# Reordering the opening of an attention-plus-MLP kernel: dummy matmuls, contiguous rows, other load order, alternating heads

## The chip, the cores and the metric

The kernel runs on one NeuronCore of a Trainium2 chip. The metric is device time in microseconds (us), median of repeated runs; every timed run here is on one core. Runs whose time lay within 1.5% of the fastest of their kernel count as fast. A single look: one run, no repeats. A difference counts as faster or slower here only beyond 2%.

The measured time of a run is some 1.8 us longer than the span that its profile draws (1246.06 against 1244.3).

## The reference

```
mod = silu(c) @ w_mod                      # c: 1x448, w_mod: 448x2688, cut in six: sa, ca, ga, sb, cb, gb
h = layernorm(x) * (1 + ca) + sa           # x: 2048x448
q = h @ wq                                 # 16 heads of 256
p = softmax(q @ k_cache^T / 16)            # per head: 2048 x 2048
x = x + ga * ((p @ v_cache) @ wo)
h = layernorm(x) * (1 + cb) + sb
x = x + gb * ((gelu(h @ w_gate) * (h @ w_up)) @ w_down)    # inner width 1792
```

Everything is bf16 in memory. K and V are inputs (a cache); only q is projected.

## The kernel before

The kernel cuts attention into 64 **units**, one for each head `h` and each row block `r` of 512 rows. A unit has 16 steps `j`, one for each 128 rows of K: two matmuls for the scores `st`, the exponential `E` on ScalarE (ACT), two matmuls for the output `oT`, and a running sum `esum` on VectorE (DVE). Scores run two steps ahead of outputs. All other work (layer norm of later row blocks, Q projections, loads, the output projection `wo`) is put into the step stream as **fills**, which are attached to a pair (u, j) of unit and step.

```
# start: loads in order. SP's queue first, then (after exp(-c)) ACT's queue
load_x(nc.sync, 0); load_wm(0, WA)              # x rows 0..511; first 960 columns of w_mod
wq[0] = load_wq(0); kTs[0] = load_k(0, parts=2) # K transposed by the DMA, in two halves
load_x(nc.sync, 2); load_wm(WA, 3 * D); wos[0] = load_wo(0)
load_x(nc.sync, 3); wq[1] = load_wq(1)
... # cps: c turned into a column by four tiny matmuls; sg = exp(-c)
load_x(nc.scalar, 1); vs[0] = load_v(0, nc.scalar)   # 1 MB of V, all at once
...
def q_proj(h, r):            # one head, one row block: 8 full matmuls
    for dc in range(2):
        qps = mi_tile([P, 512], F32, "qps")
        for ch in range(DCH):    # the fourth 128-row slice holds only 64 rows of weights
            nc.tensor.matmul(qps[:], lhsT=wq[h][:, ch, ...], rhs=hr[:, ch, :], ...)
        # half 0 copied out by DVE, half 1 by ACT
...
for t in range(4):           # row block 0
    if t == 1:
        silu_c(); modc = mod_cols(0)   # 32 tiny matmuls give sa and ca as columns
    ln.stats(t)
    if t % 2 == 1: ln.rstd(t - 1, 2)   # 1/sqrt on GpSimd (POOL)
mod_cols_out(modc, sa_c, ca1p_c)
for t in range(4): ln.norm(t)
ln.twin(nc.vector)
for pr in range(2): ln.transpose(pr)   # 16 transposes on TensorE, then modulation
q_proj(0, 0)

units = [(h, r) for h in range(H) for r in range(NC)]   # head by head
...   # row block r of head 0 needs hT of block r, so blocks 1, 2, 3 are normalised,
...   # turned (2 and 3 through DRAM) and projected inside units 0, 1 and 2
for u, (h, r) in enumerate(units):
    for j in range(NKS):
        g = u * NKS + j
        emit_st(g + 2); emit_exp(g + 1)
        ... # esum, then the two oT matmuls of step g
        for f in fills.pop((u, j), ()): f()
        if j == 7: pinv = psums()                    # 1/sum of the unit before
        if j in (9, 11, 13, 15): wo_tile(...)        # output projection of the unit before
```

The sums of a unit take a trip: `esum` goes to DRAM (`scr`), comes back transposed (`esT`), and DVE reduces it to `inv` at step 7 of the next unit.

The softmax here doesn't subtract the row's maximum and nothing guards it: scores larger than these inputs give would overflow.

## Time and profile before

| reading, kernel before | value | view |
|---|---|---|
| time, median | 1246.06 us (13 runs, 1244.86 to 1247.25) | runs |
| span of the profile | 1244.3 us | page |
| TensorE busy | 98% of the span | page |
| first score matmul starts | 14.43 us | TensorE timeline |
| last group of Q projections of heads 0 to 2 starts | 159.97 us | TensorE timeline |
| the stretch between them | 145.54 us | difference |
| from there to the end of the span | 1084.3 us | difference |

The kernel can only be faster where TensorE (PE in the profile) is idle or does work that can be dropped. The page of the kernel before, cut to the lines that say so; "9" in the clock row means 90% or more of full clock granted in that fortieth of the span:

```profile
span 1244.3 us, 17140 instructions
...
PE 1221.8 (98%) x5786; PEld 550.5 (44%) x5900; DVE 796.7 (64%) x1682; ACT 715.2 (57%) x1217; POOL 77.7 (6%) x93
...
PEclk9999999999999999999999999999999999999999
...
PE 93%; DVE 3%; issue 1%; DMA 1%; POOL 1%; ACT 0%; DVEq 0%; ACTq 0%; POOLq 0%
```

The second line is busy time by engine; the last one divides the chain of waits that ended last among the engines. PE has 93% of it. PE is idle for 22.5 us of the span (1244.3 less 1221.8); the 7% of the chain that lie elsewhere are more than that, because the chain may pass through another engine while PE is busy with something else. An upper limit for what filling holes can give is the 22.5 us, and the true one is lower: this profile lacks 114 of PE's records (5786 matmuls for 5900 weight loads), and time without a record counts as idle. The timeline of PE in the kernel before shows that start (columns: start, length, engine, source line, operation, output<-inputs, shapes, count, and in brackets the idle time before it with what ended it):

```profile
2.10 0.26 PE L167 MATMUL cps<-ones_col,c_row 1*128 1x1 bf16 x4 [2.10 <-DMA c_row<-in_c_dram]
6.70 0.24 PE L190 MATMUL modc<-scT,wm 128*128 128x1 bf16 x3 [4.33 <-DMA wm<-in_w_mod_dram]
7.19 0.93 PE L190 MATMUL modc<-scT,wm 128*128 128x1 bf16 x29 [0.25 <-DMA wm<-in_w_mod_dram]
9.13 2.49 PE L278 MATMUL tp<-id_bf,xn 128*128 128x128 bf16 x16 [1.00 <-POOL rs L232]
11.41 0.63 PE L304 MATMUL qps<-hT,wq_t 128*128 128x512 bf16 x1
12.21 2.30 PE L304 MATMUL qps<-hT,wq_t 128*128 128x512 bf16 x6 [0.17 <-ACT hT L291]
14.43 0.38 PE L345 MATMUL st<-qT,kT 128*128 128x512 bf16 x1
15.19 0.59 PE L345 MATMUL st<-qT,kT 128*128 128x512 bf16 x2 [0.38 <-ACT qT L311]
```

A lone 512-column matmul shows 0.38 us in this view, but matmuls overlap, so two take 0.59 us and follow each other every 0.216 us when the array runs at full speed (in the whole timeline twelve start one after the other from 17.13 to 19.72 us). Four of the six matmuls of the projection at 12.21 us take 1.65 us in the chain of waits, 0.41 us each: half speed, called cold below, as full speed is called warm. The clock row does not show it: it reads full from the first slice on, because it counts the time before the first clock record as full. The packed trace itself (the array `0/clock` of trace.npz) has its first record, a rise to full clock, at 13.52 us, and the last two of the six, from 13.92 us in the chain, take 0.61 us together, as two at full speed do.

After the start come holes. The waits of PE in the kernel before, from its first score matmul to 91 us (engine, line, what it waited for: sum in us, times, longest):

```profile
PE oT L538 <- DVE oTn L501: 1.0, 1, 1.0
PE st L345 <- ACT qT L311: 0.8, 2, 0.4
PE qps L304 <- DVE hT L266: 0.7, 2, 0.4
PE oT L538 <- ACT E L495: 0.5, 2, 0.3
PE st L345 <- DVE qT L309: 0.4, 1, 0.4
PE tp L278 <- POOL xn L242: 0.3, 1, 0.3
```

These are 3.7 us with a named cause. Counting the matmuls of this stretch at their full-speed spacing gave 6.0 us of holes in all (the prediction shows the count); the rest is spread in pieces for which the profile names no releaser. All of the named waits but one (0.38 us for the second half of q at 15.19) come while row blocks 1 to 3 are brought into play and head 0 is already running.

One more line of the kernel before, from the timeline of the weight loads (PEld), which are the first readers of K:

```profile
14.72 0.10 PEld L345 LDWEIGHTS <-kT 128*128 128x128 bf16 x1 [0.48 <-DMA kT<-in_A_k_cache_dram]
```

The second half-depth of K's first tile arrives at 14.7 us, just before it is wanted at 15.19. If only q were ready earlier, the scores would still wait for K (as they do for 1.49 us in before with dummies, below).

### The profile page before, as it was taken

The numbers are of one execution on the slowest core, as the hardware profiler recorded it, in microseconds if no ns is written. First come the engines' busy times: TensorE is split into PE (matmuls) and PEld (weight loads), VectorE is DVE, ScalarE is ACT, GpSimd is POOL, SyncE is SP. The second block draws the span as 40 slices with busy tenths as digits, with TensorE's granted clock in tenths as the row PEclk, the third lists the DMA queues.
The fourth block names the chain that finished last, engine by engine and source line by source line (L and its number), as shares of the span: only waits on it lengthen the run. The fifth ranks groups of instructions, "written<-read, shape, count | busy, mean of one in ns | idle before, by whom it ended". The sixth has DMA issues, their size and how long they took to land.

```text
span 1244.3 us, 17140 instructions
## 1 busy us (share of the span) xinstructions
PE 1221.8 (98%) x5786; PEld 550.5 (44%) x5900; DVE 796.7 (64%) x1682; ACT 715.2 (57%) x1217; POOL 77.7 (6%) x93
## 2 busy tenths in 40 slices
PE   7999999999999999999999999999999999999998
PEld 3444444444444444444444444444444444444443
DVE  6766666666666666676666666666666666776543
ACT  4556666666666666666666666666666666652222
POOL 4200000000000010020202010000000000000000
PEclk9999999999999999999999999999999999999999
DMA  7354031332423031402222221304041220030110
GB/s 189 87 133 97 18 67 52 47 115 51 119 43 98 22 93 43 101 18 52 63 47 67 51 67 38 81 13 97 18 86 32 49 53 18 18 85 16 50 49 16
DMA packets 181866, 76.48 MB, mean 61 GB/s; under 512 B 150161, under 2 KB 172242, under 8 KB 181778
## 3 DMA queue, kind: packets, MB, share of 16 engines
q1 hardware_dynamic: 180720, 73.87, 25.1%
q10 hardware_dynamic: 1058, 1.51, 0.4%
q8 instruction: 46, 0.75, 0.3%
q14 instruction: 42, 0.34, 0.1%
HBM read 33.67 MB, written 13.37 MB: 38 GB/s over the span
## 4 chain that ended last, share of the span: by engine, by line
PE 93%; DVE 3%; issue 1%; DMA 1%; POOL 1%; ACT 0%; DVEq 0%; ACTq 0%; POOLq 0%
PE oT L538 34%; PE st L345 34%; PE wps L354 7%; PE qps L332 6%; PE dps L592 3%; PE g_ps L579 3%; PE u_ps L579 3%; PE qps L326 1%; PE g_ps L572 1%; DVE esum L535 1%; DVE bst L224 1%; PE qps L304 0%; DMA esT<-scr 0%; DMA scr<-esum 0%; DMA x_all<-in_A_x_dram 0%
## 5 line engine op out<-in xcount | busy, mean ns | idle before, releaser
L495 ACT ACTIVATE E<-st 128x512 bf16<-128x512 f32 x1024 | 607.8, 598 | 312.3 <-PE st L345 307.0
L538 PE MATMUL oT<-E,v_h 128*128 128x512 bf16 x2005 | 599.7, 379 | 4.0 <-DVE oTn L501 1.0
L345 PE MATMUL st<-qT,kT 128*128 128x512 bf16 x2001 | 599.1, 379 | 3.9 <-ACT qT L311 0.8
L535 DVE TENSOR_TENSOR esum<-esum,E 128x512 bf16<-128x512 bf16 x896 | 396.4, 442 | 163.4 <-ACT E L495 136.4
L538 PEld LDWEIGHTS <-v_h 128*128 128x128 bf16 x2048 | 199.6, 98 | 246.2 <-DVE oTn L501 10.8
L345 PEld LDWEIGHTS <-kT 128*128 128x128 bf16 x2048 | 200.2, 98 | 228.8 <-issue 1.3
L359 DVE SCALAR_TENSOR_TENSOR x_acc<-wps,inv,x_acc 128x448 f32<-128x448 f32 x240 | 163.7, 682 | 145.3 <-PE wps L354 145.3
L354 PE MATMUL wps<-wo_t,oTn 128*128 128x448 bf16 x512 | 138.6, 352 | 0.5 <-DVE x_acc L359 0.3
L140 POOL TENSOR_TENSOR wo_t<-wo_t,ga_bf 128x448 bf16<-128x448 bf16 x32 | 34.9, 1112 | 913.1 <-DMA wo_t<-in_A_wo_dram 452.4
L584 ACT ACTIVATE gl<-g_ps 128x512 bf16<-128x512 f32 x56 | 33.4, 597 | 89.6 <-PE g_ps L579 85.5
L332 PE MATMUL qps<-hT,wq_t 128*128 128x512 bf16 x348 | 81.3, 380 | 0.6 <-issue 0.3
L354 PEld LDWEIGHTS <-oTn 128*128 128x128 bf16 x512 | 50.1, 98 | 60.9 <-issue 0.6
L337 DVE CAST qT<-qps 128x512 bf16<-128x512 f32 x60 | 41.4, 691 | 36.3 <-PE qps L332 36.1
L502 ACT CAST oTn<-oT 128x512 bf16<-128x512 f32 x64 | 37.4, 585 | 45.0 <-PE oT L538 45.0
L339 ACT CAST qT<-qps 128x512 bf16<-128x512 f32 x60 | 35.1, 585 | 46.9 <-PE qps L332 46.9
L585 DVE TENSOR_TENSOR hhT<-gl,u_ps 128x512 bf16<-128x512 bf16 x56 | 38.4, 687 | 36.1 <-PE u_ps L579 36.1
L332 PEld LDWEIGHTS <-wq_t 128*128 128x128 bf16 x360 | 32.7, 98 | 48.1 <-issue 12.7
L579 PEld LDWEIGHTS <-wgu 128*128 128x128 bf16 x336 | 30.6, 98 | 44.8 <-issue 11.9
L514 DVE TENSOR_REDUCE inv<-esT 128x4 f32<-128x512 bf16 x64 | 43.4, 679 | 4.5 <-DMA esT<-scr 4.5
L579 PE MATMUL u_ps<-hT,wgu 128*128 128x512 bf16 x165 | 45.2, 379 | 0.3
L501 DVE CAST oTn<-oT 128x512 bf16<-128x512 f32 x64 | 44.1, 689 | 0.9 <-PE oT L538 0.9
L579 PE MATMUL g_ps<-hT,wgu 128*128 128x512 bf16 x160 | 43.9, 380 | 0.8 <-issue 0.8
(71 smaller groups left out, 316.1 us busy)
## 6 DMA issues: line engine op xcount, KB each, us to landing
scr<-esum SPq DMA_DIRECT2D x64, 128.0 KB, 2.0
wo_t<-in_A_wo_dram SPq DMA_DIRECT2D x16, 224.0 KB, 6.3
wq_t<-in_A_wq_dram SPq DMA_DIRECT2D x16, 192.0 KB, 5.1
xscr<-xn SPq DMA_DIRECT2D x6, 512.0 KB, 2.9
out_dram<-ob SPq DMA_DIRECT2D x16, 112.0 KB, 1.7
wd<-in_B_w_down_dram SPq DMA_DIRECT2D x2, 784.0 KB, 4.8
x_all<-in_A_x_dram SPq DMA_DIRECT2D x3, 448.0 KB, 4.4
wgu<-in_B_w_gate_dram SPq DMA_DIRECT2D x1, 1344.0 KB
```

Source lines behind the costliest of these rows:

```text
L332: nc.tensor.matmul(qps[:], lhsT=wq[h][:, ch, dc * P:(dc + 1) * P], rhs=hT[("a", r)][:, ch, :], start=False, stop=(ch == 2),)
L337: nc.vector.tensor_copy(out=qTs[(h, r)][:, dc, :], in_=qps[:])
L345: nc.tensor.matmul(st[:], lhsT=kTs[h][:, dc, j * P:(j + 1) * P], rhs=qTs[(h, r)][:, dc, :], start=(dc == 0), stop=(dc == 1),)
L354: nc.tensor.matmul(wps[:], lhsT=oTn[:, dc, t * P:(t + 1) * P], rhs=wos[h][:, dc, :], start=(dc == 0), stop=(dc == 1),)
L359: nc.vector.scalar_tensor_tensor(out=x_acc[r][:, t, :], in0=wps[:], scalar=inv[:, t:t + 1], in1=prev[:, t, :], op0=ALU.mult, op1=ALU.add,)
L495: nc.scalar.activation(out=E[:], in_=sts.pop(g)[:], func=ACTF.Exp, scale=inv_sqrt_dh)
L501: nc.vector.tensor_copy(out=oTn[:, 0, :], in_=oT[0][:])
L514: nc.vector.tensor_reduce(out=inv[:], in_=esT[:], axis=mybir.AxisListType.X, op=ALU.add)
L535: nc.vector.tensor_tensor(out=esum[:], in0=esum[:], in1=E[:], op=ALU.add)
L538: nc.tensor.matmul(oT[i][:], lhsT=vs[h][:, j, i * P:(i + 1) * P], rhs=E[:], start=(j == 0), stop=(j == NKS - 1),)
L579: nc.tensor.matmul(ps[fc, i][:], lhsT=wgu[:, 3 * i + ch, fc * P:(fc + 1) * P], rhs=hr[:, ch, :], start=False, stop=(ch == 2),)
L585: nc.vector.tensor_tensor(out=hhT[:, fc, :], in0=gl[:], in1=ps[fc, 1][:], op=ALU.mult)
```

## The change

It means to shorten the start and fill the holes, in five parts that were made together:

1. **Dummy matmuls** on a zero tile keep the array busy while it waits for c and w_mod, so that the clock is up when the transposes and the projection come (measured: it rises at 7.04 us in after, at 13.52 in before). The first Q projection becomes six full matmuls and two with 64 rows each (64 are all that the last slice has), which read different halves of the 128 partitions.
2. **Rows**: each partition reads four adjacent rows of x instead of every 128th; the output is written the same way. Order on DVE at the start: silu first, two of the four norms before the modulation columns are copied.
3. **Loads**: ahead of K only half of V is queued, on ACT's queue, instead of x1 and all of V; x1 goes between the halves of K; x2, later parts of w_mod and wo of head 0 move into fills; K and V of head 1 come at once; two loads are issued by POOL.
4. **Order of units**: heads 0 and 1 alternate, so a new row block is needed only every two units, and one packed group projects both heads.
5. **Exp ahead of fills**: the next exponential is issued before the fills of a step, not after.

```diff
+    def spin(n):
+        for _ in range(n):
+            nc.tensor.matmul(zps[:], lhsT=wz[:, 0:P], rhs=wz[:], start=True, stop=True)
+    spin(3)                        # before cps; then spin(11) before mod_cols(0), spin(2) after,
+                                   # spin(2) twice among and after the transposes
...
-            out=x_bf[r], in_=x2d[r * 512:(r + 1) * 512, :].rearrange("(t p) d -> p t d", p=P)
+        v = x2d[r * 512:(r + 1) * 512, :].rearrange("(p t) d -> p t d", p=P)
...
-    load_x(nc.scalar, 1)
-    vs[0] = load_v(0, nc.scalar)
+    v_part(vs[0], 0, 0, NKS // 2, nc.scalar)
+    k_part(kTs[0], 0, 0, SK // 2)
+    load_x(nc.sync, 1)
+    k_part(kTs[0], 0, SK // 2, SK)
+    v_part(vs[0], 0, NKS // 2, NKS, nc.sync)
+    wq[1] = load_wq(1)
+    kTs[1] = load_k(1)
+    vs[1] = load_v(1)
...
-    units = [(h, r) for h in range(H) for r in range(NC)]
+    units = [(h, r) for r in range(NC) for h in range(2)]
+    units += [(h, r) for h in range(2, H) for r in range(NC)]
...
+    for r in range(1, NC):
+        fill(2 * r - 1, 12, lambda r=r: q_two(((0, r), (1, r))))
...
+            if (u, j) in fills:
+                emit_exp(g + 2)
             for f in fills.pop((u, j), ()):
                 f()
```

(The words behind # are a summary, not code. Cut: the helpers for the parts of K and V, the projection helpers, the new places of the other fills.)

## The prediction

> **What bounds it now.** TensorE. The page shows PE busy 98% of a 1244.3 us span; the chain of waits that ended last is 93% PE. In the steady part two attention units (head, 512 rows) take 33.89 us (Q projections in the chain at 160.57 and 194.46), against 33.7 us of matmuls at 0.216 us each. The change barely touches that or the MLP. Only edges can move:
>
> - Start: the first score matmul begins at 14.43 us (PE timeline), the second waits for qT until 15.19. Before it PE waits 2.1 us for c, 4.6 for w_mod, 1.0 for POOL's reciprocal root; the eight Q projection matmuls run from 11.41 at about 0.43 us apiece, a cold clock. [...]
> - First four units: 14.43 to the Q projection at 90.63 is 76.2 us; counting matmuls at 0.216 us (0.189 for 448 columns) gives my estimate of 70.2. So 6.0 us are holes; the list of waits names POOL's xn 0.3, exp 0.5, qT 1.2, hT 0.7, oTn 1.0.
>
> **What the change does.** (1) Dummy matmuls fill the early idle, so transposes and projection should run warm; eight projection matmuls become six full and two half-row ones side by side. (2) Each partition reads four adjacent rows of x; silu goes first; two norms precede the modulation copies. (3) Ahead of K the queues carry half of V instead of V plus x1: 1 MB less, 3 to 4 us at the 250-300 GB/s of the DMA row. K landing at 14.7 us would otherwise cap the gain. (4) The first two heads alternate, so a new hT is needed only every two units, and row blocks 1 to 3 project both heads in one packed group. (5) The next exp is issued before each fill.
>
> Start, estimated from the trace's durations: w_mod lands 7.1, mod columns done 8.1 (0.93), copies 8.75, last norms 9.4 (0.33 each), copy and transposes 10.0, hT from 10.6 (DVE 0.54, ACT 0.78 each), projection done 12.4, qT copies (0.69, 0.58, parallel) 13.15. First scores at 13.2, both halves together: gain 1.2 us.
>
> Of the 6.0 us of holes I expect 2 to remain (DVE late for oTn in unit 1, where four stats, two qT copies and four x_acc pile up; wo scaling on POOL, 2.3 us, just ahead of its reader; ACT copies). Gain 4.0. Fewer projection matmuls: about 0.5. All is on PE, hence critical. Total 5.7 us.
>
> **Predicted: 1240.5 us, range 1237.5 to 1243.5 (8 in 10).** Faster by over 2%: 0.01; within 2%: 0.98; slower: 0.01.
>
> **What would show it.** First score matmul at 12.5 to 14 us, qT halves not apart; projection matmuls at 0.216 us. PE holes inside the first four units under 2.5 us. Two-unit period later still 33.9; MLP unchanged. The gain is whole by 95 us.
>
> **What would make it wrong.** The eleven dummies, if cold, end near 7.3 us and delay the mod columns; w_mod, K or x1 landing late; x3 and w_mod now issued from POOL arriving late and blocking DVE in order; K of head 2, now loaded one unit before use instead of four, landing after its 13 us of slack (issue to landing 5 to 8); wo of head 0 scaled too late. Each costs 0.5 to 3 us.

(1.2 us at the start, 4.0 of holes and 0.5 of projections make the 5.7.)

## The result, and the profile after

| | before | after |
|---|---|---|
| time, median (range) | 1246.06 us (1244.86 to 1247.25, 13 runs) | 1239.99 us (1239.61 to 1240.40, 9 runs) |
| span of the profile | 1244.3 | 1238.1 |
| a: first score matmul | 14.43 | 13.34 |
| b: last projections of heads 0 to 2 | 159.97 | 153.45 |
| b − a (the stream of the first eight units) | 145.54 | 140.11 |
| end of span − b | 1084.33 | 1084.65 |

The ratio is 0.9952 (95% interval 0.9943 to 0.9961), which is within 2%. A ratio here is the mean time of one kernel's fast runs over that of the other's of the same rounds, so it isn't quite the ratio of the medians quoted. The medians differ by 6.07 us and the two profiled spans by 6.2 us.

The same lines of the page after:

```profile
span 1238.1 us, 17193 instructions
...
PE 1224.9 (99%) x5805; PEld 551.2 (45%) x5920; DVE 795.4 (64%) x1687; ACT 716.0 (58%) x1220; POOL 74.5 (6%) x88
...
PE 97%; DVE 1%; issue 1%; DMA 1%; ACT 0%; DVEq 0%; ACTq 0%
```

PE's idle time fell by 9.3 us, from 22.5 to 13.2, but the span only by 6.2: PE's busy time rose by 3.1 us, although its useful work fell, because the dummies count as busy and lie on the chain (6.8 us of its first 16). (This profile too lacks some 115 records. Between two profiles without gaps, before with the exponential ahead of fills and after with the rows of before, idle time falls from 15.7 to 7.6 us and busy time rises by 1.7.) A busy share cannot tell useful work from filler. The start in the timeline of PE after:

```profile
2.83 4.61 PE L168 MATMUL zps<-wz 128*128 128x512 bf16 x11
7.28 0.94 PE L204 MATMUL modc<-scT,wm 128*128 128x1 bf16 x32
...
8.51 0.61 PE L402 MATMUL tp<-id_bf,xn 128*128 128x128 bf16 x8
...
9.39 0.65 PE L402 MATMUL tp<-id_bf,xn 128*128 128x128 bf16 x8
...
10.53 1.71 PE L328 MATMUL qps<-hT,wq_t 128*128 128x512 bf16 x6
12.17 0.39 PE L322 MATMUL qps<-hT,wq_t 64*128 64x512 bf16 x2
13.34 1.45 PE L365 MATMUL st<-qT,kT 128*128 128x512 bf16 x6 [0.78 <-DVE qT L316]
```

The eleven dummies all run cold (4.61 us, 0.42 each). The transposes, 2.49 us for sixteen before, are now 0.61 and 0.65 us for eight. The first six projection matmuls take 1.71 us, where six took 2.30. The scores start in one go, six in a row; nothing waits for a second half of q. The two 64-row matmuls take 0.39 us together, as long as one full one. So the two overlap here; two full ones in a row take 0.59.

The waits of PE after, from its first score matmul to 160 us (the first of them is the wait that precedes that matmul):

```profile
PE st L365 <- DVE qT L316: 0.8, 1, 0.8
PE oT L589 <- ACT oTn L553: 0.2, 1, 0.2
```

One hole of 0.2 us has a name in 147 us. The six named ones of before are gone.

The last term: from 160 to 1080 us. First before, then after, each from its table of windows (window, its length, busy us and instruction count of PE, PEld, DVE, ACT, POOL, granted clock, DMA share, GB/s):

```profile
160.00:1080.00 920.00, 915.25 (x4258) 414.82 (x4345) 598.42 (x1253) 574.76 (x979) 44.46 (x40) 1.00 0.25 58
```

```profile
160.00:1080.00 920.00, 915.47 (x4258) 415.14 (x4343) 599.75 (x1261) 575.02 (x979) 45.01 (x42) 1.00 0.24 58
```

PE's busy time differs by 0.22 us in 920, and the time from the last mark below to the end of the span differs by 0.3. Nothing happened in the steady part. The 4.5 to 4.8 us in which PE seems idle here are missing records: the profiles of all other runs have 4344 to 4346 matmuls in this stretch and show PE busy for 919.9 to 920.0 us.

The two marks that split the gain, from the PE timelines, before and then after:

```profile
159.97 0.60 PE L326 MATMUL qps<-hT,wq_t 64*128 64x512 bf16 x4
```

```profile
153.45 0.60 PE L322 MATMUL qps<-hT,wq_t 64*128 64x512 bf16 x4
```

Both kernels have done the same eight units and nearly the same projections by then, so the subtraction is fair. The start gives 1.09 us and the stream 5.43. Of the 5.43, fewer projection matmuls are 0.48 by a count: before does three single projections of 8 matmuls (24 × 0.216 us) and three packed ones of 3.13 us, 14.57 us in all; after does one small one (1.565, half of a packed one) and four packed ones, 14.09. The timeline of after shows 3.14 us for a packed one (43.85 to 46.99 us) and 1.72 for the small one (26.31 to 28.03), so the 0.48 is an estimate. The other 4.95 us are holes: 6.0 before by the prediction's count, so about 1.0 left, of which the list of waits names 0.2. Part of that 1.0 may be an error of the count: in the profile of after with the rows of before, which lacks no record, PE is busy for 139.88 of the same 140.11 us. The end gives back 0.3 us (1084.65 against 1084.33).

### The profile page after: what moved, and what is told of

It is laid out like the page before. It is cut to its first block, busy times and chain, and to the rows that moved or that the text cites. A ratio compares the mean times of both kernels' runs of the same rounds, so it can differ in the third digit from the quotient of the medians.

```text
span 1238.1 us, 17193 instructions
## 1 busy us (share of the span) xinstructions
PE 1224.9 (99%) x5805; PEld 551.2 (45%) x5920; DVE 795.4 (64%) x1687; ACT 716.0 (58%) x1220; POOL 74.5 (6%) x88
## 4 chain that ended last, share of the span: by engine, by line
PE 97%; DVE 1%; issue 1%; DMA 1%; ACT 0%; DVEq 0%; ACTq 0%
PE st L365 35%; PE oT L589 35%; PE wps L374 8%; PE qps L328 7%; PE dps L645 3%; PE g_ps L632 3%; PE u_ps L632 3%; PE qps L322 1%; PE g_ps L625 1%; PE zps L168 1%; DMA esT<-scr 0%; DMA scr<-esum 0%; DVE esum L586 0%; DVE x_acc L379 0%; PE modc L204 0%
## 5 line engine op out<-in xcount | busy, mean ns | idle before, releaser
L328 PE MATMUL qps<-hT,wq_t 128*128 128x512 bf16 x371 | 87.1, 380 | 0.6
L146 POOL TENSOR_TENSOR wo_t<-wo_t,ga_bf 128x448 bf16<-128x448 bf16 x32 | 34.0, 1080 | 886.6 <-DMA wo_t<-in_A_wo_dram 452.6
L316 DVE CAST qT<-qps 128x512 bf16<-128x512 f32 x64 | 44.2, 691 | 40.0 <-PE qps L328 36.6
```

The source lines that it names most:

```text
L316: nc.vector.tensor_copy(out=qTs[(h, r)][:, dc, :], in_=qps[:])
L328: nc.tensor.matmul(qps[:], lhsT=wq[h][:, ch, dc * P:(dc + 1) * P], rhs=hT[("a", r)][:, ch, :], start=start, stop=stop,)
```

## The experiments

Twelve runs of ten kernels were made, each next to runs of the kernel before on the same chip. Two marks, the first score matmul (a) and the last projections of heads 0 to 2 (b), split each of them as above. This table is the main result; the sections below say what each row tells apart.

| kernel | median us | a | b − a | span − b |
|---|---|---|---|---|
| before | 1246.06 | 14.43 | 145.54 | 1084.3 |
| after | 1239.99 | 13.34 | 140.11 | 1084.7 |
| after, no dummies (three profiles) | 1243.65, single 1241.9 and 1243.66 | 14.13, 15.12, 14.77 | 140.11, 140.12, 142.01 | 1085.1, 1085.0, 1085.2 |
| after, eight dummies for eleven | 1241.99 | 16.11 | 140.11 | 1086.3 |
| after, early loads of before | 1241.60 | 14.01 | 140.87 | 1085.0 |
| after, rows of before | 1240.09 | 13.29 | 140.11 | 1084.9 |
| after, exp not ahead of fills | 1240.46 | 14.01 | 140.48 | 1084.7 |
| before, exp ahead of fills | 1246.37 | 15.15 | 145.11 | 1084.4 |
| before, with dummies | 1249.54 | 15.69 | 145.96 | 1084.9 |
| after, heads in turn, stream of before | 1249.14 | 13.30 | 148.11 | 1086.0 |

(The two other kernels with heads in turn are told in the text.) The column b − a reads 140.11 in every kernel with the full new stream, a warm array and K on time, which shows how well this mark repeats. The column a does not: it moves by itself with the clock and with the landing of w_mod. In the two rows with 1086 us and more at the end, the sums of a late unit came back late from their trip through DRAM: after 1080 us DVE waits 4.5 us for `esT` in both (2.9 in before and after), and PE then 1.2 us for DVE's x_acc.

### The dummies

**After without dummies.** Theory A: the dummies gain because they raise the clock for the transposes, the projection and the first scores. Rival B: the new order alone would do it, and the dummies cost as much as they gain.

```diff
     def spin(n):
-        for _ in range(n):
-            nc.tensor.matmul(zps[:], lhsT=wz[:, 0:P], rhs=wz[:], start=True, stop=True)
+        return
```

> The changed kernel without any dummy matmul. Theory A (the dummies warm the array): the eight projection matmuls are spaced about 0.43 us instead of 0.22, but they also wait for hT, which arrives between 10.5 and 11.5 us, so the first scores come 1.0 to 1.5 us later (14.3 to 14.9) and the time is about 1241.2. Theory B (the projection only waits for hT, the clock does not matter): first scores at 13.3 to 13.6, time within 0.4 us of the changed kernel (1240.0). Also read: when w_mod lands, which the dummies hide.

Measured: 1243.65 us median (1240.97, 1244.17, 1243.63, 1243.67), ratio to before 0.9974 (0.9960 to 0.9989). The run that was profiled is the fastest, 1240.97 us, so its profile doesn't show what the others lost.

> The kernel without dummies once more, one look. Its four times were 1240.97 (the profiled one, in which the array warmed at about 13 us) and three at 1243.6 to 1244.2. Theory A [...]: in a slow execution scores and output matmuls still run at 0.43 us for several us after 14 us, 3 us more in all. Theory B (something else is slow): matmuls at 0.216 us from 14 us on also in an execution of 1243.6. An execution of 1241 again tells nothing.

This look gave 1241.9 us, the first score at 15.12 us.

> A third look at the kernel without dummies, for its spread of times (1240.97, 1241.9, three at 1243.6 to 1244.2). Theory A [...]: in a slow one matmuls run at 0.43 us beyond 14 us. Theory B: they run at 0.216 from there, and the time is lost elsewhere, for instance to w_mod landing later.

This one gave 1243.66 us, so it caught the common case. Its PE timeline:

```profile
8.09 2.17 PE L397 MATMUL tp<-id_bf,xn 128*128 128x128 bf16 x16
10.68 2.77 PE L323 MATMUL qps<-hT,wq_t 128*128 128x512 bf16 x6 [0.42 <-DVE hT L288]
13.38 0.61 PE L317 MATMUL qps<-hT,wq_t 64*128 64x512 bf16 x2
14.77 2.72 PE L360 MATMUL st<-qT,kT 128*128 128x512 bf16 x6 [0.78 <-DVE qT L311]
17.28 1.06 PE L584 MATMUL oT<-E,v_h 128*128 128x512 bf16 x2
18.14 0.85 PE L360 MATMUL st<-qT,kT 128*128 128x512 bf16 x2
18.82 0.59 PE L584 MATMUL oT<-E,v_h 128*128 128x512 bf16 x2
```

Six scores take 2.72 us where after needs 1.45, and a pair of outputs 1.06 us where 0.59 is the warm value: the array is at half speed until about 18.6 us. In the other two looks the same kernel was warm from about 12.5 and from about 14.5 us. The clock records of the packed traces say the same: rises at 12.54, 14.17 and 18.64 us, against 7.04 in after. So the clock is the cause, theory A holds, and the moment of the rise differs by 6 us between runs of one kernel. That can explain the spread of the times without dummies, 3.2 us against 0.8 after. It is not shown that it explains every spread: before with dummies, below, was warm early in its profile, and its times still lie 3.2 us apart.

The cost of the dummies can be read too. Without them, the second part of w_mod landed at 7.2 to 7.3 us in the three looks. In the profile of after, where all eleven ran cold, they ended at 7.44 and the columns started behind them. So they cost at most 0.2 us there, for a gain of one to four us.

**After with eight instead of eleven dummies.** If eleven end only just before w_mod, eight should suffice, unless what counts is how long the array is kept busy.

```diff
-    spin(11)
+    spin(8)
```

> The changed kernel with eight dummies in place of eleven in the long row, so that they end about 1.3 us earlier (near 6.2 us, cold) than w_mod lands (7.1). Theory A (the dummies must last until the next work[...]): projection cold in some executions, times from 1240 to 1243 with a spread over 1.5 us. Theory B ([...] eleven only delay the columns): 1239.5 to 1240.2 with a spread under 1 us.

Measured: 1241.99 us (1240.3 to 1244.16), ratio 0.9970 (0.9955 to 0.9984); against after's 0.9952 the mean is worse, and the spread is 3.9 us. Not all of that is the clock's: of the 4.4 us by which the span of the profiled run, the slowest, exceeds after's (1242.5 against 1238.1), 2.8 lie before the first score and 1.6 at the end, where the sums came back late (see the table). From the PE timeline of the profiled run:

```profile
2.84 3.60 PE L168 MATMUL zps<-wz 128*128 128x512 bf16 x8
...
8.03 0.94 PE L204 MATMUL modc<-scT,wm 128*128 128x1 bf16 x29 [0.36 <-DMA wm<-in_w_mod_dram]
...
9.64 1.06 PE L402 MATMUL tp<-id_bf,xn 128*128 128x128 bf16 x8
```

Eight dummies end at 6.44 us. Then PE is idle until 7.43, and the transposes are still cold: 1.06 us for eight, against 0.61. Here w_mod landed 0.7 us later than usual as well, so part of the late start (16.11 us) isn't the clock's. Some 2.1 us of it are: in after without the exponential ahead of fills the second part of w_mod was just as late (8.02 us), the array was warm, and the scores started at 14.01.

With eight dummies the array was busy from 1.25 to 6.44 us, 5.2 us; with eleven and the columns from 1.25 to 8.2 us, 7.0 us. In all eight profiles of kernels with eleven dummies the array was warm by 8.8 us, even where w_mod came late and cut the stretch (there the rise had come during the dummies). With eight it was cold in the one profile there is. The clock records of the packed traces sharpen this. The rise came at 5.03 to 7.45 us in the eight profiles, 3.8 to 6.2 us after the first dummy, and at 14.05 us with eight dummies. In the first try with heads in turn (below) the clock rises at 7.45, falls at 48.41 and rises again at 55.23 us. What sets these moments, and how long a busy stretch must be to raise the clock for certain, was not shown; nine or ten dummies were not tried.

**Before with dummies.** Does the start gain the same without the rest of the change?

```diff
             silu_c()
+            spin(11)
             modc = mod_cols(0)
+            spin(2)
...
     for pr in range(2):
         ln.transpose(pr)
+        spin(2)
```

(Cut: the definition of `spin`, and `spin(3)` ahead of the column of c.)

> The kernel before with the dummy matmuls alone. Theory A (dummies warm the array for the projection and make the start the same in each execution): projection matmuls at 0.22 us, first scores 0.3 to 0.8 us earlier, capped by K landing at about 14.7 us; time 1244.5 to 1245.5, and a spread under 1 us where the kernel before has 2.7. Theory B (only the spread or only the mean moves): one of the two stays.

Measured: 1249.54 us (1248.34 to 1251.52), ratio 1.0030 (1.0015 to 1.0045). It is 0.3% slower than before, which neither theory had expected, and the spread is 3.2 us where theory A had said under 1. The projection did get warm: five matmuls took 1.24 us, and the first half of q was there at about 14.1 us, the second at 14.8. But the scores then waited for K. The PE timeline of this kernel:

```profile
15.69 0.39 PE L354 MATMUL st<-qT,kT 128*128 128x512 bf16 x1 [1.49 <-DMA kT<-in_A_k_cache_dram]
16.42 1.25 PE L354 MATMUL st<-qT,kT 128*128 128x512 bf16 x5 [0.34 <-DMA kT<-in_A_k_cache_dram]
```

K's first tile was complete at 16.4 us, 1.7 us later than in before (14.7), with the same loads in the same queues. What delayed it stays open. The DMA engines moved 235 GB/s on average between 7 and 16 us, against 269 in before. ACT issued x1 0.5 us later because its exponential of c had to wait for three dummies, but that this shift slows K was only argued. What is shown: dummies alone don't help this kernel, and in its profile K holds up the start by 1.3 us against before (15.69 against 14.43). The rest is not explained: that profile is of the fastest run, its span is 2.2 us over before's, and the other three runs are slower still by 1.0 to 3.2 us. The slowest of them shows a mean granted clock of 0.996, so in it the clock fell again somewhere (in the first try with heads in turn, below, a mean of 0.997 goes with one fall of 6.8 us).

### The early loads

**After with the early loads of before**: x1 and all of V on ACT's queue, ahead of K. Theory A: K then lands later than q and caps the start. Rival B: K doesn't matter.

```diff
-    v_part(vs[0], 0, 0, NKS // 2, nc.scalar)
+    load_x(nc.scalar, 1)
+    v_part(vs[0], 0, 0, NKS, nc.scalar)
     k_part(kTs[0], 0, 0, SK // 2)
-    load_x(nc.sync, 1)
     k_part(kTs[0], 0, SK // 2, SK)
-    v_part(vs[0], 0, NKS // 2, NKS, nc.sync)
```

> The changed kernel with x1 and the whole of V again in ACT's queue ahead of K. Theory A (K would have capped the gain): the first half of K lands at about 14.5 to 15, the first scores wait for it and start 1 to 2 us later, time about 1241.5. Theory B (K has slack): first scores stay at 13.3, time 1240.0.

Measured: 1241.60 us (1241.40 to 1241.83), 1.6 us over after; ratio 0.9962 (0.9948 to 0.9977). The PE timeline of this kernel:

```profile
14.01 0.39 PE L364 MATMUL st<-qT,kT 128*128 128x512 bf16 x1 [1.50 <-DMA kT<-in_A_k_cache_dram]
14.97 1.25 PE L364 MATMUL st<-qT,kT 128*128 128x512 bf16 x5 [0.58 <-DMA kT<-in_A_k_cache_dram]
```

Theory A holds. V and x1 were queued by ACT, K by SP, and K still paid: the scores waited 1.50 and 0.58 us for it. Queuing loads on another engine did not keep them out of K's way here. Of the 1.5 us, some 0.8 would have gone to waiting for q, as in after. Together with before-with-dummies it shows that for the start parts 1 and 3 of the change need each other: the dummies bring q earlier, the shorter queue brings K earlier, and the start is the later of the two.

### The rows

**After with the rows of before**, for x and for the output. Theory A: adjacent rows make the first load land earlier. Rival B: they change nothing that counts.

```diff
-        v = x2d[r * 512:(r + 1) * 512, :].rearrange("(p t) d -> p t d", p=P)
+        v = x2d[r * 512:(r + 1) * 512, :].rearrange("(t p) d -> p t d", p=P)
```

> The changed kernel with the old row layout of x and of the output (each partition reads four rows that lie apart, 896 bytes each). Theory A (four adjacent rows speed up the loads that open the kernel): x0 and w_mod land 0.3 to 1 us later, first scores later by as much, time 1240.3 to 1241. Theory B (no effect): x0 lands within 0.15 us, time 1240.0. [...]

Measured: 1240.09 us (1239.96 to 1240.38), ratio 0.9954 (0.9938 to 0.9971), with 0.9952 for after. DVE's first read of x came at 4.44 us instead of 4.30, and the first score at 13.29 instead of 13.34. B holds: the part is worth nothing measurable. The 0.14 us that x comes earlier don't reach the first score. It also clears the new layout of the some 0.6 us that after lost at its end (see below).

### The exponential ahead of fills

**After without it** (kept only at step 15, where before had it too). Theory A: it fills a good part of the holes. Rival B: it is worth little.

```diff
-            if (u, j) in fills:
+            if (u, j) in fills and j == NKS - 1:
                 emit_exp(g + 2)
```

> The changed kernel with the exp no longer issued ahead of a fill, except at the end of a unit as before. Theory A (ACT copies of a fill delay the exp that the next output matmul reads): holes of 0.3 to 0.5 us at each of the four projections of the first units and at the two transposes, together 1.0 to 2.5 us, time about 1241.5. Theory B (PE has slack enough): under 0.4 us, time 1240.0 to 1240.4.

Measured: 1240.46 us (1239.86 to 1240.87), 0.5 us over after; ratio 0.9953 (0.9938 to 0.9968). The stream took 140.48 us, 0.37 more, and one new hole appeared in the PE timeline:

```profile
26.92 0.59 PE L589 MATMUL oT<-E,v_h 128*128 128x512 bf16 x2 [0.20 <-ACT E L546]
```

**Before with it alone:**

```diff
+            if (u, j) in fills:
+                emit_exp(g + 2)
             for f in fills.pop((u, j), ()):
```

> The kernel before with one line added: exp issued ahead of each fill. Theory A (the exp order is a main part of the gain in the stream): holes of the first four units fall from 6.0 by 1 to 2 us, time about 1244.5. Theory B (it is a small part, as the changed kernel without it lost 0.36 us at one place): time within 0.7 us of the kernel before.

Measured: 1246.37 us (1246.27 to 1246.80) with 1245.65 for before on that chip, ratio 1.0004 (0.9989 to 1.0019). The exp holes did go: its stream is 145.11 us, 0.43 less than before. But the waits for hT, 0.7 us before, became the largest item in the list of PE's waits:

```profile
PE qps L304 <- DVE hT L266: 1.5, 3, 0.9
```

B holds in both directions: some 0.4 us on the stream, with or without the rest of the change.

### The order of units

By subtraction, about 4.5 of the 4.95 us of holes should belong to the alternation of heads with its packed projections (4.95 less 0.4 for the exponential). Three kernels tried to undo the alternation alone.

**First try**: heads one after the other, row blocks 1 to 3 projected singly inside units 0 to 2 as in before, everything else as in after.

```diff
-    units = [(h, r) for r in range(NC) for h in range(2)]
-    units += [(h, r) for h in range(2, H) for r in range(NC)]
+    units = [(h, r) for h in range(H) for r in range(NC)]
...
-        fill(2 * r - 1, 12, lambda r=r: q_two(((0, r), (1, r))))
+        fill(r - 1, 13, lambda r=r: q_one(0, r))
+    fill(1, 15, lambda: q_two(((1, 0), (1, 1))))
+    fill(3, 15, lambda: q_two(((1, 2), (1, 3))))
...   # x2, x3 loaded early, the norms of blocks 2 and 3 in units 0 and 1, as in before
```

> The changed kernel with the heads one after the other again (four row blocks of head 0, then head 1; Q projections of head 0 one by one, x2 and x3 loaded early as before); start, row layout and early exp kept. Theory A (alternating the two heads removes the holes on hT, qT and oTn): holes of about 2.5 to 3.5 us come back in the first three units, time about 1243. Theory B (issuing exp before the fill removes most holes): under 1 us comes back, time about 1240.5. First scores at 13.3 in both.

Measured: 1252.94 us (1251.83 to 1253.24), ratio 1.0051 (1.0034 to 1.0068), 13 us over after and far beyond the expectation. The PE timeline shows why:

```profile
48.76 0.53 PE L376 MATMUL wps<-wo_t,oTn 128*128 128x448 bf16 x1 [4.92 <-POOL wo_t L146]
```

The scaling of wo by ga sits on POOL, and in this order it was queued behind POOL's norms of row block 3, so PE waited 4.92 us, then 0.51 more. The clock then fell: until about 55.6 us each pair of matmuls took 1.06 instead of 0.59 us. The table of windows of this kernel, 49 to 56 us, has a granted clock (third value from the right) of 0.55:

```profile
49.00:56.00 7.00, 6.50 (x18) 2.31 (x17) 5.98 (x10) 1.79 (x3) 4.47 (x5) 0.55 0.60 168
```

This kernel doesn't measure the alternation; it measures a misplaced fill. The long wait cost twice here: 4.92 and 0.51 us of waiting, and the half-speed stretch after it.

**Second try**: the same with wo, its scaling and x2, x3 loaded early, in the order of before.

```diff
+    load_x(nc.sync, 2)
     v_part(vs[0], 0, NKS // 2, NKS, nc.sync)
+    load_wm(nc.sync, WA, 3 * D)
+    wos[0] = load_wo(0, nc.sync)
+    load_x(nc.sync, 3)
...
+    fill(1, 0, lambda: mod_rep(2, ga_bf))
+    fill(1, 1, lambda: scale_wo(wos[0]))
```

> Heads one after the other again, as in the run before, but with the load and the scaling of the first wo back at their early places, so that POOL does not scale it behind the norms of row block 3 (that run lost 5.4 us of waiting there, and ran at half clock after it). Theory A (alternating the heads removes the holes on qT, hT and oTn): 2.5 to 3.5 us of holes remain in the first three units against 0.7 in the changed kernel, time 1242.5 to 1243.5. Theory B (the early exp and DVE's norms did it): under 1 us, time 1240 to 1241.

Measured: 1249.33 us (1249.16 to 1249.53), ratio 1.0027 (1.0011 to 1.0044). The clock stayed up, but about 7 us of holes remained by name; the largest sum was 3.0 us of scores waiting for DVE's copies of qT, in four waits. DVE also did the norms of row block 1 here, which POOL does in before.

**Third try**: with those norms on POOL again, the order of units, norms and projections is that of before, under the new start and the new loads (the exponential ahead of fills and the smaller single projection stay).

```diff
-    add_ln(("a", 1), ..., at(0, 1, 2, 3, 4), at(0, 5, 6, 7, 8), at(0, 10, 11))
+    add_ln(("a", 1), ..., at(0, 0, 1, 2, 3), at(0, 3, 3, 3, 3), at(0, 10, 11), on_pool=True)
```

> Start and loads of the changed kernel, and behind them the stream exactly in the order of the kernel before: heads one after the other, row block 1 normalized on POOL as before (in the run before this, DVE had those norms beside the stats of row block 2 and lost 7 us of holes); the early exp stays. Theory A (the interleaving of the first units is worth about 5 us): holes of 5 to 6 us as in the kernel before, first scores at 13.3, time 1244.5 to 1245.5. Theory B (the start brings most of the gain in the stream too, by later needs for data): holes under 2 us, time 1241 to 1242.

Measured: 1249.14 us (1247.47 to 1249.77), ratio 1.0024 (1.0009 to 1.0039). The stream that cost 145.54 us in before costs 148.11 here. The largest hole of PE, in its timeline:

```profile
48.62 0.38 PE L332 MATMUL qps<-hT,wq_t 128*128 128x512 bf16 x1 [2.64 <-DVE hT L284]
```

It is named after DVE's modulation of hT. The DVE timeline of the same kernel shows what DVE was waiting for before that:

```profile
47.03 0.69 DVE L564 TENSOR_REDUCE inv<-esT 128x4 f32<-128x512 bf16 x1 [5.97 <-DMA esT<-scr]
```

and the same instruction in the DVE timeline of before:

```profile
44.88 0.69 DVE L514 TENSOR_REDUCE inv<-esT 128x4 f32<-128x512 bf16 x1 [1.57 <-DMA esT<-scr]
```

The sums of unit 0 come back late from their trip through DRAM. From issuing the write of `esum` to issuing the transposed read took 4.31 us (40.08 to 44.39) instead of 2.14 (40.17 to 42.31). In DVE's program and timeline the modulation of the new row block (from 48.16 us) stood behind the sums, and PE's projection behind the modulation. The hole cost twice here too: the table of windows shows a granted clock of 0.50 from 49.5 to 52.9 us. Why the trip takes longer stays open. The obvious candidate is contention with K and V of head 1, which are loaded early here; the DMA engines were indeed busier before it (a share of 0.73 against 0.25 from 30 to 36 us), but not during it (0.29 against 0.39 from 40 to 44.4 us). In after, which has those early loads too, PE waits for no hT at all. It has one such slow write of `esum` as well, 4.0 us from issue to landing at 84.07 us, but PE waited for nothing there (its list of waits above).

So all three expectations failed in size: undoing the order under the new start and loads costs 9.1 to 13.0 us, more than the whole change gains. The old order of units with the old loads is faster (1246.06 us) than with the new ones (1249.14), so the order and the loads must be judged together. What the alternation is worth with the old load order was not run and stays open; 4.5 us is a remainder, not a measurement.

## Why the prediction was right

The prediction was 1240.5 us; the median is 1239.99. Point by point:

- **What bounds the kernel**: right. PE's busy time in the steady 920 us stayed equal within 0.22 us, the time behind mark b within 0.3, and all of the gain came before 160 us.
- **Start, 1.2 us**: right. The first score came at 13.34 us (13.2 predicted), a gain of 1.09, with six scores in a row. The removals show its parts: without the shorter queue ahead of K the kernel is 1.6 us slower, without dummies 1.0 to 4.2 us depending on the run. The parts don't add up to 1.2, because the start is the latest of several arrivals, and because a late clock also slows the first scores behind the mark (six in 2.72 us in the third look without dummies, 1.45 in after).
- **Dummies end near 7.3 us if cold**: they ended at 7.44, at a cost of at most 0.2 us.
- **K would otherwise cap the gain**: right. In after with the early loads of before the first scores wait for K; in before with dummies they do too, but there K also landed later than in before.
- **Holes, gain 4.0 with 2 left**: the mis-sized term. It measured 4.95, with about 1.0 left. The holes that were feared in unit 1, DVE late for oTn, the scaling of wo on POOL, ACT's copies, showed as one wait of 0.2 us. K of head 2 and the loads issued by POOL made PE wait for nothing.
- **Projection, 0.5 us**: 0.48 by the count.
- **Total 5.7 us**: 6.07 by the medians, 6.2 by the profiles. The terms measured 1.09 + 4.95 + 0.48 = 6.52 in the profiles, less 0.3 at the end. Of that end, the last addition on DVE comes 0.23 us earlier relative to mark b, and the time from it to the end of the span is some 0.6 us longer (3.7 against 3.2 us). The last write of the output is not the reason: it lands 1.7 us after its issue in every profile. The loss lies behind that landing, among the closing instructions, and it isn't chance: the time from the last addition to the end is 3.7 to 3.8 us in all seven profiles with the new order and the new loads, with either row layout, 3.2 to 3.3 in the six with heads in turn, and 3.5 in after with the early loads of before. So it comes with the change of program; what in it does so stays open.
- **Gain whole by 95 us**: close. At 104.04 us after is at the point that before reaches at 113.79 (the modulation matmuls in the fifth step of unit 5). Less one packed projection of 3.13 us that after hasn't done yet, that is 6.6 us.

Two things the prediction missed. It treated the cold clock as a fixed cost, whereas the moment of the rise differs by microseconds from run to run (12.54 to 18.64 us in three looks without dummies); taking that lottery out may be why after's times lie within 0.8 us, which no run shows by itself. And it listed the parts as if they were separable; the runs show that the dummies added alone to the kernel before, and the new start and loads without the new order, each give a kernel slower than before.

## What to carry to other kernels

At the start of a kernel, list when each input of the first matmul is ready and work on the latest; bringing one forward (here q, by a warm clock) pays only until the next one (here K) caps it: before with dummies waited 1.49 us for K. Where dummies are used to raise the clock, keep the array busy as long as the wait allows rather than for the shortest time that once worked, and judge it by the spread of several runs, not by one profile: here eleven dummies gave times within 0.8 us, eight within 3.9. An order of fills that was tuned to one set of load times can lose with another (here 1246.06 us became 1249.14), so after moving loads look first at the small round trips that an engine waits for, and at the work that stands behind them on the same engine.

## Further measurements

- The moment at which the clock rises: in eight profiles whose dummies start alike at 1.25 us the clock records put it at 5.03 to 7.45 us, 2.4 us apart. In three looks at one kernel without dummies it came at 12.54, 14.17 and 18.64 us, 6 us apart. Why was not shown.
- The busy stretch: 5.2 us of dummies was not enough in the one profile of it; eleven dummies were in all eight profiles, with the rise 3.8 to 6.2 us after the first of them.
- The clock records agree with the spacing of the matmuls (rise at 13.52 us in before, 7.04 in after), also for a half-speed stretch in the middle of a kernel (48.41 to 55.23 us in the first try with heads in turn). What misleads is the view of the profile: its clock row reads 1.00 for the first 15 us of the kernel before, where projections ran at 0.41 us apiece, because there is no record before the first rise.
- The pair of 64-row matmuls took 0.39 us, but here the next full one started 0.33 us after the start of the pair (27.70 to 28.03 us), not 0.216; for two pairs in a row it was 0.54 us (43.85 to 44.39).
- The landing of one and the same load varies. K's first tile was complete at 14.7 us in before and at 16.4 in the same kernel with dummies. The writes of the output take 1.7 us from issue to landing by their median, but one of the 16 took 2.4 us in after and 2.7 in after with the rows of before; one write of `esum` took 4.0 in after, where their median is 2.0.
